# Attention and feed-forward on one core: the second layer's M1 copied to a second bank pair and accumulated on, early value products and the first pair's normalising at other places

## The chip, the cores and the metric

One core of one Trainium2 chip runs the whole kernel. The metric is the device time of one execution in microseconds, as the median of several runs; less is better.

## The reference, cut to what matters

```python
# q, k, v: (batch 8, heads 8, seq 576, head_dim 64)
scores = q @ k.T / 8
# heads 0-3 see 0 <= i-j < 32; heads 4-7 see 0 <= i-j < 128 with (i-j) % 4 == 0
attn = softmax(where(mask, scores, -1e9))
x = (attn @ v).transpose(0, 2, 1, 3).reshape(4608, 512)
h = x @ w_in                            # 512 -> 2048
g = 0.5 * h * (1 + erf(h / sqrt(2)))    # gelu
out = g @ w_out                         # 2048 -> 512
```

## The kernel before, in words

The 4608 tokens are nine chunks of 512. Attention makes the x of a chunk in four pieces (`part` 0 to 3: qk loads, scores, exp, sums, normalising, a transposition `turned` that is partly done by DMA, the value products, and `xout`, which writes x). All matmuls of the feed-forward layers take each operand as a high part rounded to the fp32r format and a low remainder, and issue three terms (high x high, low x high, high x low).

Chunks 0, 1 and 2 go through the two layers directly: `ffn_h_part` (matmul at line 604) for x @ w_in into PSUM bank 4 or 5, `ffn_gelu` (gelu on ACT at L611, a cast of the high part on ACT at L106, a subtraction on DVE for the low part), and `ffn_o` (matmul at L627) into banks 0 to 3. Their order is a string written by hand, `SCHEDULE` (lines 51 to 73): a word such as `h0.2` stands for one step (feature block 0, part 2), `av0.2` for the value products of chunk 0 (`av_wide`, matmul at L500), `scores1.0` for those of L292 and L306, `av1.3` for L518, `o10` for the twelve L627 matmuls of feature block 10, `split2`, `rest2`, `high2` for cutting the weights of block 2 into high and low parts. The word `:a` or `:d` says which engine takes the step.

Chunks 3 to 8 go in three pairs, (3,4), (5,6) and (8,7), by a scheme of seven products in place of eight blocks. Each pair has four units (a quarter of the weights each), and each unit has 28 products: 14 of the first layer (H), then 14 of the second (O), M1 to M7 in two halves each. A product is six matmuls of 128x128 on 128x512 (line 1036, `product`). Weight pieces come through a ring of five tiles filled by DMA (`ring_load`, L991, issued on SP). The first layer's operands B11, B21, B22, T1 to T4 are made by `combine` (casts on ACT at L915, subtractions on DVE at L920). In the second layer, `operands` does the same from the gelu outputs: casts of the high parts on ACT (L1082), low parts on DVE (L1083), and the differences T1 (L1084), T3 (L1085), T2 (L1086) and T4 (L1087) on DVE. `first_layer` makes the gelu inputs (L1065 and L1068 on DVE) and runs the gelu on ACT (L1066, L1067, L1069); line 1061 copies the first layer's M1 to a second bank.

[...] In the second layer the seven products of a unit rotate over three bank pairs, `OBANKS`: M1 in (0,1), M3 in (2,3), M5 in (4,5), M2 in (0,1), M7 in (2,3), M6 in (0,1), M4 in (4,5). Each is drained by `drains` on DVE (L1096 copies for the first unit, L1098 adds to the SBUF totals for the later ones), seven drains per unit, each of 128x1024. After a pair's last unit `final` combines the seven totals by seven additions (L1112; on POOL for the first two pairs, on DVE before the closing unit of the last pair) and sends outT by DMA from SP (L1109). The very last unit, the closing one, has an order and drains of its own (`last_drains`), and already copies and accumulates.

Every step of the paired part is entered by `add(at, rank, step)` at a time in ticks (one tick is one product); `upto` emits them by time, then rank, between the products. An engine runs its instructions in the order in which they are emitted; SP is the queue from which nearly all DMAs are issued, in that order. For the pieces of the next pair's attention, `attend` takes a dict of times, `begin` for the first pair's first piece.

Of the kernel before, what the change touches and what calls it, by code (L numbers as in the profile page):

```python
# [39 lines left out]
BANK0 = (4, 0, 2, 6)  # L40

# [15 lines left out]
turn0.3 half0.2.0:a half0.2.1:a av0.0 half0.3.1:a high0.1:d half0.3.0:a rest1 w2 qk1.0 high1:a rest1 x0.0:a x0.1:a  # L57
x0.0 x0.1 av0.2 x0.2:a h0.0 h0.1 x0.3:a x0.2 qk1.1 h1.0 h1.1 x0.3 h0.2 h0.3 mid3 split2 h0 split2 h1.2 split2 w3
h1.3 rest2 h0:a scores1.0 rest2 high2:a h0 h1 h1:a h2 split3 w4 mid5 low1.0 split3 o0 low1.0:a h2 split3 mid4 h2:a
# [8 lines left out]
rest12 turn1.3:a h10 turn1.2:a high12:d join13.1 rest12 av1.2 h11 split13 mid14 h11:a split13 h12 av1.3   # L68
h11 x1.2:a join15.0 w14 x1.2 split13 o10 x1.3:a h12 x1.3 h12:a keep0 rest13 join15.1 h12 o11 rest13 high13:a
# [17 lines left out]
def attn_ffn(ctx: ExitStack, tc: tile.TileContext, qk, qk_lp, qk_ld, v, v_ld, w, outT):  # L87
    nc = tc.nc
# [402 lines left out]
    def av_wide(s, o):  # L491

        yield "p"
        for a in range(2):
            for r in range(4):
                c0 = (2 * r + a) * 2 * KB
                for y, g, e, cols in sorted([(y, *x) for y in (s, o) for x in parted(y)], key=lambda x: (x[2], x[1])):
                    t = y.t[:, (2 * (g % 2) + a) * 4 + r]
                    bank = BANK0[s.p + e] + 1
# [219 lines left out]
    for token in SCHEDULE.split():  # L719
# [3 lines left out]
        if name == "fill":  # L723
            bank = 7
# [178 lines left out]
    def combine(c, z, at):  # L903
# [34 lines left out]
        B11=(0, -13, -12.4), B21=(0, -11.5, -10.9), T1=(-8.6, -7.8, -7), B22=(0, -2.4, -1.6), T3=(-4.6, -3.8, -3.2), T2=(-5.4, -4.9, -4.2),  # L938
        T4=(-3.5, -3, -2.5)).items()})
# [58 lines left out]
    SLOT = dict(B11=0, T3=0, B22=1, T2=1, T1=2, T4=2, B21=3)  # L998
# [314 lines left out]
```

## Time and profile before

| what | value |
|---|---|
| time of three runs | 855.35, 856.35, 861.83 us; median 856.35 us |
| the profiled execution | 852.99 us, of which the span of instructions is 851.1 us |
| mean granted TensorE clock over the span | 0.992 |
| instructions in the span | 19932 |
| busy share PE, DVE, ACT, POOL | 96%, 72%, 55%, 12% |

PE is the matmul engine (TensorE), PEld its weight loads, DVE the vector engine, ACT the scalar engine, POOL GpSimd, SP the engine that issues DMAs. "idle before" is the time in which an engine had nothing to run ahead of a group of rows, and behind the arrow stands what ended it; "issue" means that no semaphore event of the profile explains the wait. One counting rule matters below: an instruction of the program on plain fp32 operands (lines 306, 500, 518 and 572) runs as two matmuls in the trace, so 64 such instructions of the order are 128 of the trace. Those of lines 292, 604, 627 and 1036 count alike in both. Each matmul of the trace has one weight load beside it.

### The profile page before, as it was taken

How to read it: one execution, taken by the hardware profiler on the slowest of the kernel's cores; microseconds unless marked ns; L12 is line 12 of the kernel's file. 1: busy time of each engine (PE TensorE's matmuls, PEld its weight loads, DVE VectorE, ACT ScalarE, POOL GpSimd, SP SyncE). 2: the span in 40 equal slices, each digit the busy share in tenths (PEclk: the TensorE clock that was granted, in tenths of full speed). 3: DMA queues.
4: the chain of work that ended last, by engine and by line, in shares of the span. 5: the costliest groups of instructions: out<-in, count | busy, mean ns of one | idle time of the engine just before them, and what ended most of it. 6: DMA issues, size and time to landing. Idle time of an engine off the chain costs nothing.

```text
span 851.1 us, 19932 instructions
## 1 busy us (share of the span) xinstructions
PE 817.4 (96%) x8400; PEld 664.3 (78%) x8400; DVE 615.8 (72%) x703; ACT 465.7 (55%) x1089; POOL 103.0 (12%) x94
## 2 busy tenths in 40 slices
PE   6799989999998999899999999999999999999997
PEld 5587868887786888788888877787888777888885
DVE  7597962435765579585959799966767898483977
ACT  7477823454766357473737574646665635244242
POOL 2000002052302630000000018000000064000000
PEclk9999999999999999999999999999999999999999
DMA  9997367984599847967777777876667668566664
GB/s 359 418 418 281 115 199 298 382 302 154 206 332 349 317 160 254 317 223 235 249 225 264 235 273 227 282 261 200 213 204 234 204 206 269 182 195 195 197 197 150
DMA packets 118295, 212.30 MB, mean 249 GB/s; under 512 B 6848, under 2 KB 92864, under 8 KB 110784
## 3 DMA queue, kind: packets, MB, share of 16 engines
q1 hardware_dynamic: 118064, 210.79, 71.7%
q8 instruction: 66, 1.08, 0.5%
q10 hardware_dynamic: 144, 0.26, 0.1%
q14 instruction: 21, 0.17, 0.1%
HBM read 161.21 MB, written 42.99 MB: 240 GB/s over the span
## 4 chain that ended last, share of the span: by engine, by line
PE 73%; DVE 11%; DMA 7%; issue 3%; ACT 3%; SPq 2%; DVEq 0%; ACTq 0%
PE ps L1036 40%; PE ps L604 14%; PE ps L627 12%; DMA turned<-turned 3%; PE ps L306 2%; DVE g L1083 2%; PE ps L572 2%; DMA raw_w<-w 2%; DMA outT<-o_sb 1%; DVE acc L1098 1%; DVE xc L920 1%; DMA v_sb<-v 1%; SPq L382 1%; PE ps L529 1%; DMA ring<-wd 1%
## 5 line engine op out<-in xcount | busy, mean ns | idle before, releaser
L1036 PE MATMUL ps<-xc,ring 128*128 128x512 f32 x1008 | 239.2, 395 | 0.0
L1036 PE MATMUL ps<-g,ring 128*128 128x512 f32 x1008 | 233.3, 391 | 0.8 <-DVE g L1083 0.7
L1036 PEld LDWEIGHTS ps<-xc,ring 128*128 128x128 f32 x1008 | 189.8, 190 | 41.8 <-DVE acc L1098 0.6
L1036 PEld LDWEIGHTS ps<-g,ring 128*128 128x128 f32 x1008 | 188.1, 188 | 43.3 <-DVE g L1083 3.4
L1083 DVE TENSOR_TENSOR g<-g_value,g 128x1024 fp32r<-128x1024 f32 x84 | 106.5, 1277 | 75.9 <-ACT g L1082 75.9
L604 PE MATMUL ps<-x,weight 128*128 128x512 f32 x576 | 138.0, 394 | 2.0 <-issue 2.0
L627 PE MATMUL ps<-g,weight 128*128 128x512 f32 x576 | 137.0, 395 | 1.5 <-issue 1.5
L627 PEld LDWEIGHTS ps<-g,weight 128*128 128x128 f32 x576 | 108.5, 190 | 25.3 <-issue 2.4
L604 PEld LDWEIGHTS ps<-x,weight 128*128 128x128 f32 x576 | 107.2, 188 | 25.6 <-issue 2.9
L1082 ACT CAST g<-g_value 128x1024 fp32r<-128x1024 f32 x84 | 87.1, 1046 | 36.9 <-DVE g_value L1084 20.1
L1112 POOL TENSOR_TENSOR acc<-acc 128x1024 f32<-128x1024 f32 x14 | 44.2, 3169 | 348.2 <-DVE acc L1098 347.7
L616 DVE TENSOR_TENSOR g<-gf,g 128x512 fp32r<-128x512 f32 x48 | 34.3, 715 | 61.2 <-ACT g L106 61.2
L1098 DVE TENSOR_TENSOR acc<-ps,acc 128x1024 f32<-128x1024 f32 x56 | 67.5, 1217 | 13.6 <-PE ps L1036 13.6
L427 ACT ACTIVATE sm<-sm,st 128x64 f32<-128x64 f32 (+1 forms) x224 | 75.4, 338 | 0.2
L611 ACT ACTIVATE gf<-ps 128x512 f32<-128x512 f32 x48 | 28.7, 598 | 81.1 <-PE ps L604 81.0
L783 POOL TENSOR_TENSOR whole<-weight 128x512 f32<-128x512 f32 x32 | 47.2, 1508 | 134.0 <-DMA sd<-sums 54.5
L1061 ACT COPY ps<-ps 128x512 f32<-128x512 f32 x24 | 13.7, 570 | 78.2 <-PE ps L1036 78.2
L1057 ACT COPY u<-ps 128x512 f32<-128x512 f32 x48 | 28.1, 586 | 32.9 <-PE ps L1036 29.3
L427 ACT ACTIVATION_READ_ACCUMULATOR sm<-sm,st 128x1 f32 x224 | 42.1, 188 | 0.0
L920 DVE TENSOR_TENSOR xc<-xn,xc 128x1024 fp32r<-128x1024 f32 x21 | 34.9, 1682 | 8.5 <-ACT xc L915 8.5
L1066 ACT ACTIVATE g_value<-g_value 128x512 f32<-128x512 f32 x24 | 15.1, 632 | 44.6 <-DVE g_value L1065 44.6
L306 PEld LDWEIGHTS ps<-raw_qk 64*32 64x32 f32 x2304 | 26.2, 110 | 12.0 <-issue 4.0
(124 smaller groups left out, 792.6 us busy)
## 6 DMA issues: line engine op xcount, KB each, us to landing
ring<-sd SPq DMA_DIRECT2D x96, 512.0 KB, 4.3
ring<-wd SPq DMA_DIRECT2D x72, 512.0 KB, 4.3
v_sb<-v SPq DMA_DIRECT2D x17, 1024.0 KB, 7.2
raw_qk<-qk SPq DMA_DIRECT2D x32, 512.0 KB, 7.6
wd<-weight SPq DMA_DIRECT2D x16, 1024.0 KB, 10.1
sd<-sums SPq DMA_DIRECT2D x16, 1024.0 KB, 6.0
raw_w<-w SPq DMA_DIRECT2D x15, 1024.0 KB, 17.1
weight<-wd SPq DMA_DIRECT2D x8, 1024.0 KB, 8.6
```

The source lines that it names most:

```text
L306: nc.tensor.matmul(s.sc[32 * r:32 * r + 32, h, c0:c0 + s.nk], x[:, q0:q0 + 32], x[:, k0:k0 + s.nk], start=s.c > 1, stop=s.c > 1 or u == NU ...
L427: nc.scalar.activation(t, s.sc[:, h, at:at + 2 * KB] if s.c < 2 else t, AF.Exp, bias=st[:, 0], scale=SCALE if s.c < 2 else -1.0, accum_out ...
L604: nc.tensor.matmul(bank, weights[f][:, t, cc * P:(cc + 1) * P], x[:, xx], start=n == 1 and i == 0, stop=n == parts and i == 2)
L616: nc.vector.tensor_sub(g[:, 1], gf, g[:, 0])
L627: nc.tensor.matmul(ps[:, d], weights[f][:, t, DM + d * P:DM + (d + 1) * P], gs[f][:, u], start=f == first and n == 0, stop=f == last and n ...
L783: nc.gpsimd.tensor_add(to, x, y)
L920: nc.vector.tensor_sub(combined[k][:, :, 1], part(*VALUE[k]), combined[k][:, :, 0])
L1036: nc.tensor.matmul(ps[:, bank], lhs, rhs, start=start and i == 0, stop=i == 5, skip_group_check=True)
L1082: add(base + t, 4, run("a", lambda k=k, v=v: nc.scalar.copy(operand(k, 0, final), val(v))))
L1083: add(base + t1, 4, run("d", lambda k=k, v=v: sub(operand(k, 1, final), val(v), operand(k, 0, final))))
L1098: plus(total(m), src, total(m))
L1112: add(base + dt * n, 6, run(e[n], lambda g=g, to=to, x=x, y=y: g.tensor_add(total(to), total(x), total(y))))
```

## The change

Four things are done, all on the order of work and the banks; the values computed are the same.

1. In the hand-written `SCHEDULE`, twelve of the first L604 matmuls (h0.0, h0.1, h1.0, h1.1) go ahead of `av0.2`, `scores1.0` goes ahead of the next L604 matmuls, and splits of weight block 2 go ahead of `x0.2`. The bank of chunk 0's wide value products is taken from a table of its own, `XBANK0`.
2. In the same string `av1.3` goes behind `o10`.
3. The normalising of the first pair's first attention piece goes from 0.2 to -2.8 ticks, and three low parts of `combine(3, 4)` go from before tick 0 to ticks 1.6, 3.2 and 5.
4. In the second layer of every unit but the closing one, ACT copies M1 from banks (0,1) to (2,3); M2 is accumulated on that copy and M6 on M1 itself. M1 has no drain of its own any more; six drains stay. The order of the products becomes M1, M3, M2, M5, M6, M7, M4, their operands are made in another order, and `final` has five additions in place of seven; the total of M2 needs none and is sent out by itself, at two ticks before the additions.

```diff
+XBANK0 = (5, 1, 3, 2)
@@ SCHEDULE, around the first L604 matmuls
-turn0.3 half0.2.0:a half0.2.1:a av0.0 half0.3.1:a high0.1:d half0.3.0:a rest1 w2 qk1.0 high1:a rest1 x0.0:a x0.1:a
-x0.0 x0.1 av0.2 x0.2:a h0.0 h0.1 x0.3:a x0.2 qk1.1 h1.0 h1.1 x0.3 h0.2 h0.3 mid3 split2 h0 split2 h1.2 split2 w3
-h1.3 rest2 h0:a scores1.0 rest2 high2:a h0 h1 h1:a h2 split3 w4 mid5 low1.0 split3 o0 low1.0:a h2 split3 mid4 h2:a
+turn0.3 half0.2.0:a half0.2.1:a av0.0 half0.3.1:a high0.1:d half0.3.0:a rest1 w2 qk1.0 qk1.1 high1:a rest1 x0.0:a
+x0.1:a x0.0 x0.1 h0.0 h0.1 h1.0 h1.1 split2 av0.2 x0.2:a split2 x0.3:a split2 scores1.0 x0.2 x0.3 h0.2 h0.3 mid3
+h0 h1.2 w3 h1.3 rest2 h0:a rest2 high2:a h0 h1 h1:a h2 split3 w4 mid5 low1.0 split3 o0 low1.0:a h2 split3 mid4 h2:a
@@ SCHEDULE, the last value products of chunk 1
-rest12 turn1.3:a h10 turn1.2:a high12:d join13.1 rest12 av1.2 h11 split13 mid14 h11:a split13 h12 av1.3 
-h11 x1.2:a join15.0 w14 x1.2 split13 o10 x1.3:a h12 x1.3 h12:a keep0 rest13 join15.1 h12 o11 rest13 high13:a
+rest12 turn1.3:a h10 turn1.2:a high12:d join13.1 rest12 av1.2 h11 split13 mid14 h11:a split13 h12
+h11 join15.0 w14 split13 o10 av1.3 x1.2:a h12 x1.2 x1.3:a h12:a x1.3 keep0 rest13 join15.1 h12 o11 rest13 high13:a
@@ the first pair
-        begin = H01 if j else dict(qk=-17, scores=-10, low=-9.6, exp=(-7.8, -6.2), every=.2, norm=0.2, swap=2.1, v=-3, av=9.2, back=(9.6, 10.4))
+        begin = H01 if j else dict(qk=-17, scores=-10, low=-9.6, exp=(-7.8, -6.2), every=.2, norm=-2.8, swap=2.1, v=-3, av=9.2, back=(9.6, 10.4))
-        B11=(0, -13, -12.4), B21=(0, -11.5, -10.9), T1=(-8.6, -7.8, -7), B22=(0, -2.4, -1.6), T3=(-4.6, -3.8, -3.2), T2=(-5.4, -4.9, -4.2),
-        T4=(-3.5, -3, -2.5)).items()})
+        B11=(0, -13, -12.4), B21=(0, -11.5, -10.9), T1=(-8.6, -7.8, -7), B22=(0, -2.4, 3.2), T3=(-4.6, -3.8, 1.6), T2=(-5.4, -4.9, -4.2),
+        T4=(-3.5, -3, 5)).items()})
@@ the second layer of the pairs
-    OSEQ = tuple((m, e) for m in ("M1", "M3", "M5", "M2", "M7", "M6", "M4") for e in range(2))
+    OSEQ = tuple((m, e) for m in ("M1", "M3", "M2", "M5", "M6", "M7", "M4") for e in range(2))
-    A, B_, C = (4, 5), (0, 1), (2, 3)
-    OBANKS = (B_, C, A, B_, C, B_, A)
+    FIRST, COPY, OTHER = (0, 1), (2, 3), (4, 5)
+    OBANK = dict(M1=FIRST, M3=OTHER, M2=COPY, M5=OTHER, M6=FIRST, M7=COPY, M4=OTHER)
-    SLOT = dict(B11=0, T3=0, B22=1, T2=1, T1=2, T4=2, B21=3)
+    SLOT = dict(B11=0, T2=0, B22=1, T3=1, T1=2, B21=3, T4=3)
@@ operands
-            plan = [("B11", 7.5, 8.5), ("B22", 11.1, 11.9), ("T1", 13.2, 15.2), ("B21", 15.1, 16.4), ("T3", 16.2, 18.4), ("T2", 18.3, 20.3), ("T4", 20.6, 22.4)]
-            at = (12.6, 13.3, 14.9, 18.2)
+            plan = [("B11", 7.5, 8.5), ("B22", 11.1, 11.9), ("B21", 14.9, 15.9), ("T1", 14.2, 17.1), ("T2", 16.4, 18.8), ("T3", 18.2, 20.8), ("T4", 20.2, 22.4)]
+            at = (12.6, 14.4, 14.9, 17.6)
@@ drains
-        for n, b in enumerate(OBANKS):
-            m = OSEQ[2 * n][0]
+        for e in range(2):
+            add(base + 15 + e, 2, run("a", lambda e=e: nc.scalar.copy(ps[:, COPY[e]], ps[:, FIRST[e]])))
+        for n, m in enumerate(("M3", "M2", "M5", "M6", "M7", "M4")):
...
-            add(base + (16, 18, 23, 22, 24, 26, 28)[n], 2, run("d", fn))
+            add(base + 18 + 2 * n, 2, run("d", fn))
-    FINAL = (("M2", "M1", "M2"), ("M6", "M1", "M6"), ("M7", "M6", "M7"), ("M6", "M6", "M5"), ("M5", "M7", "M5"), ("M3", "M6", "M3"), ("M4", "M7", "M4"))
+    FINAL = (("M5", "M5", "M6"), ("M3", "M3", "M5"), ("M6", "M6", "M7"), ("M4", "M4", "M6"), ("M5", "M5", "M7"))
@@ final
+        if pair:
+            add(base - 2, 6, run("q", lambda: out("M2")))
@@ the loop over the products
-            bank, start = OBANKS[(k - QT // 2) // 2][y], True
+            bank, start = OBANK[x][y], x not in ("M2", "M6")
```

On PE, near the start: the value products of chunk 0 (L500 before, L501 in the changed file), the first-layer matmuls (L604, L605), the scores of chunk 1 (L292 and L306, L293 and L307) and the second layer's first matmuls (L627, L628). Before:

```order
L500 MATMUL ps<-zeroed,v_sb 32x64 x128
L604 MATMUL ps<-x,weight 128x512 x24
L292 MATMUL ps<-early 128x256 x2
L306 MATMUL ps<-raw_qk 32x64 x32
L292 MATMUL ps<-early 128x256 x2
L306 MATMUL ps<-raw_qk 32x64 x32
L604 MATMUL ps<-x,weight 128x512 x12
L627 MATMUL ps<-g,weight 128x512 x24
```

and with the change:

```order
L501 MATMUL ps<-zeroed,v_sb 32x64 x64
L605 MATMUL ps<-x,weight 128x512 x12
L501 MATMUL ps<-zeroed,v_sb 32x64 x64
L293 MATMUL ps<-early 128x256 x2
L307 MATMUL ps<-raw_qk 32x64 x32
L293 MATMUL ps<-early 128x256 x2
L307 MATMUL ps<-raw_qk 32x64 x32
L605 MATMUL ps<-x,weight 128x512 x24
L628 MATMUL ps<-g,weight 128x512 x24
```

Half of the value products now stand behind twelve first-layer matmuls, and the scores stand ahead of the other 24 instead of between 24 and 12.

On SP, at the start of the first pair: outT stores of chunk 2, the DMA swaps that finish the transposition (`turned`, L382 before, L383 in the changed file) and loads of the weight ring (L991). Before:

```order
L641 DMA outT<-o_sb 128x512 x3
L382 DMA turned<-turned 32x512 x2
L991 DMA ring<-sd_139 128x4x256
L382 DMA turned<-turned 32x512 x4
L991 DMA ring<-wd_1_134 128x4x256
L382 DMA turned<-turned 32x512 x2
L991 DMA ring<-wd_0_133 128x4x256
```

and with the change:

```order
L642 DMA outT<-o_sb 128x512 x2
L383 DMA turned<-turned 32x512 x2
L642 DMA outT<-o_sb 128x512
L383 DMA turned<-turned 32x512 x6
L991 DMA ring<-sd_139 128x4x256
L991 DMA ring<-wd_1_134 128x4x256
L991 DMA ring<-wd_0_133 128x4x256
```

The eight swaps, which were spread over two ring loads, stand ahead of both.

On DVE, in the second half of a unit of the third pair, which has no attention beside it: T1 (L1084), the gelu inputs (L1068), T3 (L1085), T2 (L1086), T4 (L1087), the low parts (L1083) and the drains (L1098 before, L1100 in the changed file). Before:

```order
L1084 TENSOR_TENSOR g_value<-g_value 128x1024
L1068 TENSOR_TENSOR g_value<-ps,u 128x512
L1085 TENSOR_TENSOR g_value<-g_value 128x1024
L1068 TENSOR_TENSOR g_value<-ps,u 128x512
L1086 TENSOR_TENSOR g_value<-g_value 128x1024
L1083 TENSOR_TENSOR g<-g_value,g 128x2x512
L1098 TENSOR_TENSOR acc<-ps,acc 128x1024
L1083 TENSOR_TENSOR g<-g_value,g 128x2x512
L1098 TENSOR_TENSOR acc<-ps,acc 128x1024
L1087 TENSOR_TENSOR g_value<-g_value 128x1024
L1083 TENSOR_TENSOR g<-g_value,g 128x2x512 x2
```

and with the change:

```order
L1084 TENSOR_TENSOR g_value<-g_value 128x1024
L1068 TENSOR_TENSOR g_value<-ps,u 128x512 x2
L1085 TENSOR_TENSOR g_value<-g_value 128x1024
L1086 TENSOR_TENSOR g_value<-g_value 128x1024
L1083 TENSOR_TENSOR g<-g_value,g 128x2x512 x2
L1087 TENSOR_TENSOR g_value<-g_value 128x1024
L1100 TENSOR_TENSOR acc<-ps,acc 128x1024
L1083 TENSOR_TENSOR g<-g_value,g 128x2x512
L1100 TENSOR_TENSOR acc<-ps,acc 128x1024
L1083 TENSOR_TENSOR g<-g_value,g 128x2x512
```

The drain of M1, the first L1098 before, is gone; the first drain is now that of M3, behind eight other instructions counted from T1.

## Rows read from the trace of the kernel before

**Rows 1.** The profile page: busy time of PE (share of the span, instructions), and the DMA queue of kind "instruction" (packets, MB, share of 16 engines).
```profile
PE 817.4 (96%) x8400; PEld 664.3 (78%) x8400; DVE 615.8 (72%) x703; ACT 465.7 (55%) x1089; POOL 103.0 (12%) x94
...
q8 instruction: 66, 1.08, 0.5%
```

**Rows 2.** The waits of PE over the whole span: the line that waited, what ended the wait, us in total, times, longest us.
```profile
PE ps L572 <- DMA turned<-turned: 5.0, 6, 1.8
PE ps L518 <- issue: 4.2, 2, 3.8
PE ps L500 <- issue: 3.8, 1, 3.8
...
PE ps L306 <- DVE xn L585: 1.5, 2, 0.9
...
PE ps L1036 <- DVE g L1083: 0.7, 1, 0.7
```

**Rows 3.** The timeline of PE from 22 to 46 us: start, us, engine, line, operation, tiles, shape, count, and the idle time before it.
```profile
28.09 2.73 PE L500 MATMUL ps<-zeroed,v_sb 128*32 128x64 f32 x125 [3.76 <-issue]
...
34.38 5.06 PE L604 MATMUL ps<-x,weight 128*128 128x512 f32 x21 [1.98 <-issue]
39.28 0.40 PE L292 MATMUL ps<-early 128*128 128x256 f32 x2
...
41.61 3.01 PE L604 MATMUL ps<-x,weight 128*128 128x512 f32 x12
44.46 1.75 PE L627 MATMUL ps<-g,weight 128*128 128x512 f32 x7
```

**Rows 4.** The DMA view of three stretches, 34.4 to 37.9, 37.9 to 39.0 and 111.4 to 112.4 us: queue and kind, packets, MB, share of 16 engines. In the first stretch q1 is the only queue.
```profile
q1 hardware_dynamic: 202, 1.48, 101.7%
...
q8 instruction: 1, 0.02, 6.1%
...
q8 instruction: 1, 0.02, 5.5%
```

**Rows 5.** Windows of the trace: stretch, its length, busy time and count of PE, PEld, DVE, ACT, POOL, then the granted TensorE clock (1.00 is full), the DMA share and GB/s.
```profile
29.40:32.70 3.30, 3.00 (x58) 2.02 (x46) 1.44 (x3) 2.04 (x3) 0.00 (x0) 0.50 1.02 419
...
114.80:118.10 3.30, 3.30 (x9) 2.61 (x8) 2.97 (x5) 3.27 (x6) 0.00 (x0) 0.50 0.03 5
360.50:363.80 3.30, 3.30 (x30) 2.55 (x12) 0.78 (x2) 0.00 (x0) 0.00 (x0) 0.50 0.23 79
538.00:541.30 3.30, 3.30 (x10) 2.53 (x9) 3.23 (x4) 1.37 (x3) 0.00 (x0) 0.50 1.05 383
```

**Rows 6.** The timeline of ACT from 38 us on: the gelu of feature block 0, its cast, and the cast of weight block 2.
```profile
38.12 0.60 ACT L611 ACTIVATE gf<-ps 128x512 f32<-128x512 f32 x1 [5.10 <-PE ps L604]
38.75 0.62 ACT L106 CAST g<-gf 128x512 fp32r<-128x512 f32 x1
39.27 1.17 ACT L106 CAST weight<-raw_w 128x1024 fp32r<-128x1024 f32 x1
```

**Rows 7.** The timeline of PE from 104.7 to 122 us: the value products av1.2 and av1.3 (L518) with first- and second-layer matmuls.
```profile
104.75 1.40 PE L518 MATMUL ps<-turned,v_sb 64*32 64x32 f32 x128
106.08 3.01 PE L604 MATMUL ps<-x,weight 128*128 128x512 f32 x12
...
113.87 0.61 PE L518 MATMUL ps<-turned,v_sb 64*32 64x32 f32 x43 [3.85 <-issue]
114.40 7.33 PE L627 MATMUL ps<-g,weight 128*128 128x512 f32 x24
```

**Rows 8.** The timeline of PE at the first pair's first value products (L572).
```profile
356.49 0.32 PE L572 MATMUL ps<-v_sb,turned 64*32 64x64 f32 x8
357.22 0.44 PE L572 MATMUL ps<-v_sb,turned 64*32 64x64 f32 x16 [0.41 <-DMA turned<-turned]
359.48 1.37 PE L572 MATMUL ps<-v_sb,turned 64*32 64x64 f32 x104 [1.82 <-DMA turned<-turned]
```

**Rows 9.** The timeline of DVE ahead of it: low parts of `combine`, and the transposition that the swaps wait for.
```profile
340.74 3.49 DVE L920 TENSOR_TENSOR xc<-xn,xc 128x1024 fp32r<-128x1024 f32 x3
...
345.90 1.25 DVE L374 STREAM_TRANSPOSE turned<-sm 128x1024 f32<-128x1024 f32 x1
```

**Rows 10.** The timeline of SP's DMA issues in the same stretch: start, us that the issuing took.
```profile
349.61 4.12 SPq L382 DMA_DIRECT2D turned<-turned  x4
...
354.54 1.26 SPq L382 DMA_DIRECT2D turned<-turned  x2
```

**Rows 11.** The timeline of DVE in the second layer of a unit of the third pair.
```profile
749.39 1.22 DVE L1084 TENSOR_TENSOR g_value<-g_value 128x1024 f32<-128x1024 f32 x1
750.53 0.68 DVE L1068 TENSOR_TENSOR g_value<-ps,u 128x512 f32<-128x512 f32 x1
751.13 1.21 DVE L1085 TENSOR_TENSOR g_value<-g_value 128x1024 f32<-128x1024 f32 x1
```

**Rows 12.** The timeline of ACT in the same unit: the copies that follow its first two products, and two casts of operands.
```profile
733.08 0.57 ACT L1061 COPY ps<-ps 128x512 f32<-128x512 f32 x1 [9.54 <-PE ps L1036]
734.44 0.57 ACT L1061 COPY ps<-ps 128x512 f32<-128x512 f32 x1 [0.79 <-PE ps L1036]
...
753.64 2.00 ACT L1082 CAST g<-g_value 128x1024 fp32r<-128x1024 f32 x2
```

**Rows 13.** Timelines of POOL and DVE: six of the POOL additions after the first pair, one DVE instruction beside them, and the same DVE instruction at a time without POOL work.
```profile
513.91 19.06 POOL L1112 TENSOR_TENSOR acc<-acc 128x1024 f32<-128x1024 f32 x6 [2.40 <-DVE acc L1098]
...
517.51 3.21 DVE L367 TENSOR_TENSOR sm<-sm,st 128x1024 f32<-128x1024 f32 x1
...
652.27 1.23 DVE L367 TENSOR_TENSOR sm<-sm,st 128x1024 f32<-128x1024 f32 x1
```

More of the change, by code (lines that the diff above doesn't have):

```diff
@@ L498, in av_wide @@
                     t = y.t[:, (2 * (g % 2) + a) * 4 + r]
-                    bank = BANK0[s.p + e] + 1
+                    bank = XBANK0[s.p + e]
                     nc.tensor.matmul(ps[32 * g:32 * g + 32, bank, c0:c0 + 2 * KB], y.v[:, a, r, cols],
@@ L535, in xout @@
         if s.c < 2:
-            px = ps[:, s.bank + 1] if s.wide_v else ps[:, s.bank:s.bank + 2, s.p % 2 * 256:s.p % 2 * 256 + 256]
+            px = ps[:, XBANK0[s.p]] if s.wide_v else ps[:, s.bank:s.bank + 2, s.p % 2 * 256:s.p % 2 * 256 + 256]
             to = [s.x[:, t] if s.wide_v else s.x[:, t].rearrange("p (k n) -> p k n", k=2) for t in range(2)]
@@ L958, in attn_ffn @@
             (0, "M3"), (1, "M3"), (0, "M4"), (1, "M4"))
-    OSEQ = tuple((m, e) for m in ("M1", "M3", "M5", "M2", "M7", "M6", "M4") for e in range(2))
+    OSEQ = tuple((m, e) for m in ("M1", "M3", "M2", "M5", "M6", "M7", "M4") for e in range(2))
     LSEQ = tuple((m, e) for m in ("M1", "M3", "M2", "M6", "M5", "M7", "M4") for e in range(2))
-    A, B_, C = (4, 5), (0, 1), (2, 3)
-    OBANKS = (B_, C, A, B_, C, B_, A)
-    LBANKS = (B_, C, B_, C, B_, C, A)
+    FIRST, COPY, OTHER = (0, 1), (2, 3), (4, 5)
+    OBANK = dict(M1=FIRST, M3=OTHER, M2=COPY, M5=OTHER, M6=FIRST, M7=COPY, M4=OTHER)
     X_OF = dict(M1="B11", M2="B21", M3="B22", M4="T4", M5="T1", M6="T2", M7="T3")
@@ L1089, in drains, with fn @@
     def drains(base, q):
-        for n, b in enumerate(OBANKS):
-            m = OSEQ[2 * n][0]
-            def fn(b=b, m=m):
-                src = ps[:, b[0]:b[0] + 2]
+        for e in range(2):
+            add(base + 15 + e, 2, run("a", lambda e=e: nc.scalar.copy(ps[:, COPY[e]], ps[:, FIRST[e]])))
+        for n, m in enumerate(("M3", "M2", "M5", "M6", "M7", "M4")):
+            def fn(m=m):
+                b = OBANK[m][0]
+                src = ps[:, b:b + 2]
                 if q == 0:
@@ L1112, in final @@
             add(base + dt * n, 6, run(e[n], lambda g=g, to=to, x=x, y=y: g.tensor_add(total(to), total(x), total(y))))
-            if pair and to in PLACE:
+            if pair and n in (1, 3, 4):
                 add(base + dt * n + .1, 6, run("q", lambda to=to: out(to)))
@@ L1155, in attn_ffn @@
             if closing(j, q):
-                final(base + .3, 1, None, "ddddddd")
+                final(base + 1.3, 1.2, None, "ddddd")
                 last_drains(base, PAIRS[j])
@@ L1160, in attn_ffn @@
         if j < NPP - 1:
-            final(base + QT + 1, 2, PAIRS[j], "ggggggg")
+            final(base + QT + 1, 2, PAIRS[j], "ggggg")
     steps.sort(key=lambda t: t[:3])
```

## The prediction

> **What bounds the kernel now.** I began with the page: PE is busy for 817.4 of 851.1 us [rows 1]. A change of order can win only from PE's idle time and from stretches in which PE runs at half clock; what delays PE costs in full. The changed kernel issues as many matmuls as before, so the whole forecast is a count of PE's stalls. Then I read PE's waits: the largest causes are swaps of `turned` (5.0 us in 6), two "issue" waits of 3.8 us and, smaller, DVE results late for L306 and L1036 [rows 2]. Third, the timeline around each of those that the change touches [rows 3, 7, 8]. [...]
>
> The "issue" waits need a cause. Queue q8, of kind instruction, brought 66 packets of 1.08 MB together [rows 1]: 16.4 KB each, and 16,800 matmuls and loads of PE over 66 is 255 instructions for a packet, some 127 matmuls. The stalls at 28.09 and 34.38 are 125 + 3 = 128 matmuls apart (three of the 24 of L604 ran before the second) [rows 3]. In 37.9 to 39.0 and in 111.4 to 112.4 one such packet came in, and PE resumed 1.5 us after the latter, at 113.87 [rows 4, 7]; in 34.4 to 37.9 other DMAs filled the engines (101.7%) and none came [rows 4]. So I take it that one block of 128 matmuls is fetched ahead, that the fetch is asked for when the block before it is entered, and that it comes late when DMA is full. A block of L604 or L627 matmuls takes 128 x 0.24 = 31 us (0.24 is 2.85 us from 41.61 to 44.46 over 12 [rows 3]) and hides that; a block of short attention matmuls takes 2 to 3 us and does not.
>
> [...]
>
> **A. Early value products and scores: +3.5 us.** Up to 34.38 both orders use up the same two blocks, so the stalls of 3.76 and 1.98 stay. Before, the third block then held 21 long matmuls, which hid its successor's fetch. Now it holds 9 matmuls of L501 and 119 of the scores: 0.2 + 119/132 of 2.33 us (39.28 to 41.61 [rows 3]) = 2.3 us. PE stands at the block's end at 36.7, and the next block can be used at 39.0 + 1.5 = 40.5 [rows 4]: a new stall of 3.8 us. A stall of 3.76 was followed by half clock after 1.3 us [rows 3, 5], so I charge that too. After 40.5 come 13 scores (0.2) and 24 L605 (24 x 0.24 = 5.7), then 1.65 for the clock: 48.0, where PE stood at 44.46 before. The last 12 of the 24 wait for feature block 0's gelu, its cast and the weight cast, 2.32 us on ACT [rows 6] that the scores used to cover, against six matmuls now; at half clock these take 2.9 us and cover it, so it costs nothing beside the slow stretch. Bounds: no stall and full clock, but that ACT wait exposed (2.32 + 0.3 - 1.4 = 1.2), gives 34.38 + 0.2 + 2.33 + 5.7 + 1.2 = 43.8, -0.6; both losses and a fetch 1.5 us later give +6.2.
>
> **B. `av1.3` behind `o10`: -4.3 us.** Before, PE reached a block's end at 110.02, stood for 3.85 us, and ran at half clock from 114.8 [rows 5, 7]. Now 12 L628 matmuls (12 x 0.24 = 2.8 us) stand ahead of av1.3. They need only the gelu of block 10, which stands ahead of h11 in the schedule. The fetch is asked for at the same instruction, so PE arrives at 110.02 + 2.8 less the 12 value matmuls that fall behind the edge (0.15) = 112.7 and waits 1.2. That saves 2.65, and, as the stall is short, the 1.65 of half clock. Bounds: all of it gone, -5.5; the slow stretch stays and the fetch comes 1.6 us later, -1.0. The DMAs that `join15` and `w14` issue do not move past a swap.
>
> **C. First pair's normalising: -3.9 us.** PE waits 0.41 + 1.82 for swaps and then has half clock [rows 5, 8]: 3.88 us. The transposition at 345.90 stood behind three low parts (3.49 us at 340.74) [rows 9]; these now come later, and it ends near 343.7. On SP, the last swaps were issued by 355.8 behind two ring loads [rows 10]. Now the eight stand together: those at 349.61 took 1.03 each, so all are out by 343.7 + 8.2 = 351.9, and with the 3.7 us that the last took before (355.8 to 359.48) they land by 355.6, ahead of PE at 356.49. The ring load that they pass goes out 0.6 us later; no wait of PE on the ring stands in rows 2. The three low parts at 1.6 to 5 ticks serve products M3 and M4 of the unit, ticks 10 to 13. Bounds: -3.9 and 0.
>
> **D. M5 behind M3's drain: +6.8 us.** This is the new wait. M5 uses the banks of M3, two products later, and its first matmul (tick 20) waits for M3's drain; behind it stand all products, and PE has nothing else. DVE takes 1.14 us for a 128x1024 instruction (749.39 to 750.53) and 0.60 for a 128x512 one [rows 11]. From T1 at 749.39: two gelu inputs to 751.73, T3 to 752.86, T2 to 754.0. B21's low part waits for its cast on ACT (after the second gelu, some 754.5; the cast pair of before ran 753.64 to 755.64 [rows 12]). Then B21 low, T1 low and T4 end at 757.9, and the drain ends at 757.92 + 1.21 = 759.1. PE, at 1.36 us a product (733.08 to 734.44 [rows 12]), reaches tick 20 at 758.7. So 0.45 us a unit. Eleven units have this; seven plain ones 3.2 us, the other four, where DVE also runs attention and low parts of the next pair, some 0.7 to 1.0 each: 3.6. Bounds: nothing, if the queue runs 0.5 earlier, and one whole drain per unit, 11 x 1.21 = 13.3.
> The drain that goes (M1's) saves PE nothing, since DVE wasn't waited for there. The two new copies, 0.57 each [rows 12], stand behind B21's cast and end at 755.6, before M2 wants the bank at 756.2: nothing, by 0.6 us of cover.
>
> [...]
>
> **E. Fewer additions on POOL: -3.0 us.** While POOL adds (19.06 us for six [rows 13]), a DVE multiplication takes 3.21 us in place of 1.23 [rows 13]. That made L306 wait 1.5 us for DVE and was followed by half clock at 538 [rows 2, 5]: 3.2 us. Five additions that start one drain later, in place of seven, cover less of it. The 0.7 of L1036 on DVE [rows 2], beside the second pair's additions, goes too. Against that, `turned` swaps after the first pair now stand behind M2's and M3's stores on SP: 0.9 us. Bounds: -3.9, and +1.5 where the slow instructions only move.
>
> **Sum.** 3.5 - 4.3 - 3.9 + 6.8 - 3.0 = -0.9 on the profiled 852.99, so 852.1. The median of the runs before, 856.35, is 3.36 above that execution; hence 855.5. About 1% (8.5 us) is what a measurement of this kernel tells from no change.
>
> **Rivals.**
> 1. The early stalls are no fetches but belong to the instructions that stand there. For: the profile names no cause. Against: the spacing of 128 and the packets. Then A gives back 3.76 + 1.98 + 1.65 less 1.2 = -6.2, and B its 5.5 in full: 855.5 - 9.7 - 1.2 = 844.6. Chance 0.13.
> 2. M3's drain is in time, D near +1: T1 or the cast comes 0.5 us earlier. For: the miss is 0.45 in a queue of eight. Against: the queue is tied to product 13 through L1068. 849.7. Chance 0.20.
> 3. C fails: the swaps go out early and still land late, as in the other five waits on them [rows 2]. 859.4. Chance 0.09.
> 4. The slower side: DVE's queue ahead of M3's drain is one instruction longer in each unit. ACT's chain before B21's low part (two gelus, T1's cast, B21's cast) has no slack, and each 1.14 us it slips goes through T1 low, T4 and the drain to PE: 11 x 1.14 = 12.5, 868.0. It decides from 0.8 us a unit on (9.5 us over eleven). Against: ACT idles between these casts. Chance 0.12.
>
> The forecast has 0.46; its own range is 850 to 861. Faster by over 1% (below 847.8): rival 1 and 0.02 of rival 2, 0.15. Slower (above 864.9): rival 4 and 0.01 of rival 3, 0.13. Within 1%: 0.72. A range of 844.5 to 863 holds rivals 1 to 3 and the forecast, and leaves rival 4 out.
>
> **What would show it.** A: a PE wait on "issue" near 37 to 40 in the scores. B: an issue wait of about 1.2 in L519 near 113, without half clock behind. C: no wait for `turned` near 357. D: waits of L1036 on the drain (acc, DVE) of 0.3 to 1 in nearly every unit, some 6.8 together; if they are under 2, rival 2 is right, if above 15, rival 4. E: no half clock near 538. I am wrong in the cause of the early stalls if in the changed kernel they don't stand 128 matmuls apart.

## The result, and the profile after

The changed kernel is slower: 863.96 us median (861.72 to 868.18, 11 runs), against 859.21 us for the kernel before on the same chips (853.5 to 861.91, 11 runs). The ratio is 1.0069, 95% interval 1.0042 to 1.0097, some 6 us. Forecast were 855.5 us and a range of 844.5 to 863: no change that can be told, and the range missed by 1 us. Its profiled execution took 862.84 us with a span of 861.0, near its median. That of before (852.99) turned out to lie low: in later sets of 20 to 35 runs its kernel had medians of 856.5 to 861.0. The ratios here and below leave out as slow what lies over 1.5% above the fastest run of the same kernel: among the changed kernels that is one of e13's nine runs and four of e6's 12, and over all 12 e6's median is 861.40 us, against 861.02 for all runs of before beside it.

The page after: PE is busy for 5.5 us more and idle for 4.4 us more than before [rows 1].

```profile
PE 822.9 (96%) x8400; PEld 664.6 (77%) x8400; DVE 599.9 (70%) x690; ACT 475.0 (55%) x1111; POOL 91.2 (11%) x90
```

The waits of PE after, to be laid beside [rows 2]:

```profile
PE ps L573 <- issue: 5.9, 3, 3.7
...
PE ps L307 <- issue: 3.1, 1, 3.1
...
PE ps L605 <- ACT weight L107: 1.9, 2, 1.6
PE ps L1036 <- DVE acc L1100: 1.8, 4, 0.8
...
PE ps L519 <- issue: 1.4, 1, 1.4
PE ps L1036 <- ACT ps L1091: 1.4, 2, 0.7
```

Three kinds of wait are new: for a weight cast on ACT, for drains (`acc`) and for the copies of M1 (L1091). The stall of av1.3 fell from 3.85 to 1.4 us, that of L307 on DVE (`xn`, 1.5) is gone, and the value products of the pairs (L573) have issue stalls of 5.9 us, 3.7 of them in one place.

**The early part.** The timeline of PE, beside [rows 3]:

```profile
36.85 0.74 PE L307 MATMUL ps<-raw_qk 64*32 64x64 f32 x51
40.65 0.34 PE L307 MATMUL ps<-raw_qk 64*32 64x64 f32 x13 [3.06 <-issue]
40.91 4.62 PE L605 MATMUL ps<-x,weight 128*128 128x512 f32 x12
45.83 3.02 PE L605 MATMUL ps<-x,weight 128*128 128x512 f32 x12 [0.29 <-ACT weight L107]
48.68 1.52 PE L628 MATMUL ps<-g,weight 128*128 128x512 f32 x6
```

The scores run dry with 13 matmuls left, as counted from the blocks. The second layer starts at 48.68 instead of 44.46: +4.2. The stalls before it did not stay, as step A has them, at 3.76 and 1.98: the change has one of 1.46 us at 28.43 and none at the next block's edge, and runs at half clock in between (below). The stalls at 28.43 and 40.65 stand 255 matmuls apart, two blocks, so step A's sign of a wrong cause did not come.

**av1.3.** PE, beside [rows 7], and ACT in the same stretch:

```profile
115.45 0.88 PE L519 MATMUL ps<-turned,v_sb 64*32 64x32 f32 x73
117.78 0.74 PE L519 MATMUL ps<-turned,v_sb 64*32 64x32 f32 x55 [1.44 <-issue]
118.44 3.02 PE L628 MATMUL ps<-g,weight 128*128 128x512 f32 x12
123.02 3.37 PE L605 MATMUL ps<-x,weight 128*128 128x512 f32 x12 [1.56 <-ACT weight L107]
```

```profile
118.55 0.59 ACT L107 CAST x<-ps 128x512 fp32r<-128x512 f32 x1 [7.78 <-PE ps L519]
...
121.84 1.12 ACT L107 CAST weight<-raw_w 128x1024 fp32r<-128x1024 f32 x1
```

ACT stands idle for 7.78 us in front of the cast of x, which waits for av1.3, and the weight cast is queued behind it. av1.3 now ends 4 us later, so the cast does, and PE waits for it.

**The first pair's value products**, beside [rows 8], run without a wait:

```profile
360.01 1.51 PE L573 MATMUL ps<-v_sb,turned 64*32 64x64 f32 x128
```

**The second layer.** Units are counted from 0 to 11 over the three pairs. The unit of [rows 11] is unit 9. PE ran through its second layer without a gap before:

```profile
750.56 19.20 PE L1036 MATMUL ps<-g,ring 128*128 128x512 f32 x84
```

DVE and PE in that unit after:

```profile
765.60 1.22 DVE L1087 TENSOR_TENSOR g_value<-g_value 128x1024 f32<-128x1024 f32 x1
766.74 1.22 DVE L1100 TENSOR_TENSOR acc<-ps,acc 128x1024 f32<-128x1024 f32 x1
```

```profile
765.76 1.98 PE L1036 MATMUL ps<-g,ring 128*128 128x512 f32 x8
768.01 3.25 PE L1036 MATMUL ps<-g,ring 128*128 128x512 f32 x13 [0.27 <-DVE acc L1100]
```

M3's drain ends at 767.96 and M5 starts at 768.01. The unit's products 14 to 20, with this wait of 0.27 among them, take 0.43 us longer than before, and to 24 another 0.13. In units 0 to 6, where attention runs beside it, the second copy of M1 stands behind other work on ACT; this is unit 5:

```profile
594.14 0.57 ACT L1091 COPY ps<-ps 128x512 f32<-128x512 f32 x1
594.72 1.28 ACT L428 ACT_TABLE_LOAD   x1
596.02 0.35 ACT L428 ACTIVATE sm<-sm,st 128x64 f32<-128x64 f32 x1
...
596.70 0.57 ACT L1091 COPY ps<-ps 128x512 f32<-128x512 f32 x1
```

Between the two copies lies an activation table load of 1.28 us and part of a softmax, and the second half of M2 waits 0.71 for its bank. In unit 4 that wait is 0.64. In unit 0 the second copy starts at 374.73, behind a table load too, and ends at 375.31; M2's second half starts at 375.35, 0.17 us late, and M2 takes some 0.3 us more in all.

**A stall that nobody forecast**, at the value products of the second pair's third attention piece, first before, then after:

```profile
622.81 1.73 PE L572 MATMUL ps<-v_sb,turned 64*32 64x64 f32 x128
```

```profile
625.42 1.46 PE L573 MATMUL ps<-v_sb,turned 64*32 64x64 f32 x124
630.61 0.30 PE L573 MATMUL ps<-v_sb,turned 64*32 64x64 f32 x4 [3.73 <-issue]
```

The DMA view of the changed kernel in 621.0 to 628.1 and in 628.1 to 629.4 us (queue, packets, MB, share):

```profile
q1 hardware_dynamic: 1742, 1.79, 80.2%
...
q8 instruction: 1, 0.02, 5.2%
```

The first stretch holds no instruction packet. It came only when most of the other traffic was over (q1 at 5.7% of the second stretch), at 628.1 or later; PE went on at 630.61. In the kernel before, a packet came in 618.3 to 619.9, ahead of the same value products. The granted clock after:

```profile
27.80:34.50 6.70, 6.07 (x98) 4.84 (x102) 2.43 (x3) 0.00 (x0) 0.00 (x0) 0.50 1.02 419
41.50:44.70 3.20, 3.20 (x9) 2.47 (x8) 0.00 (x0) 1.17 (x3) 0.00 (x0) 0.50 1.02 420
115.00:118.40 3.40, 1.96 (x131) 1.49 (x129) 0.00 (x0) 0.00 (x0) 0.00 (x0) 1.00 0.35 142
...
632.00:635.20 3.20, 3.20 (x9) 2.50 (x8) 1.38 (x3) 0.63 (x1) 0.00 (x0) 0.50 0.27 74
```

```profile
533.00:536.30 3.30, 3.30 (x74) 2.65 (x67) 0.78 (x2) 0.00 (x0) 0.00 (x0) 0.50 0.99 313
```

Beside [rows 5]: no half clock behind av1.3 any more, but one at 533 behind a swap wait of 1.6 us in place of the one at 538, a new one at 632 behind the new stall, and 6.7 us of it in the early part in place of 3.3.

### The profile page after: what moved, and what is told of

Read it like the earlier page. It is cut to its first block, busy times and chain, and to the rows that moved or that the text cites. A ratio compares the mean times of both kernels' runs of the same rounds, so it can differ in the third digit from the quotient of the medians.

```text
span 861.0 us, 19923 instructions
## 1 busy us (share of the span) xinstructions
PE 822.9 (96%) x8400; PEld 664.6 (77%) x8400; DVE 599.9 (70%) x690; ACT 475.0 (55%) x1111; POOL 91.2 (11%) x90
## 4 chain that ended last, share of the span: by engine, by line
PE 70%; DVE 13%; ACT 7%; DMA 4%; issue 3%; SPq 1%; DVEq 0%; ACTq 0%
PE ps L1036 38%; PE ps L605 14%; PE ps L628 12%; PE ps L307 3%; DVE g L1083 2%; DMA turned<-turned 2%; PE ps L573 2%; ACT g L1082 1%; ACT sm L428 1%; DMA raw_qk<-qk 1%; DVE acc L1100 1%; DMA v_sb<-v 1%; SPq L383 1%; DVE g_value L1084 1%; DVE g_value L1087 1%
## 5 line engine op out<-in xcount | busy, mean ns | idle before, releaser
L1036 PE MATMUL ps<-g,ring 128*128 128x512 f32 x1008 | 237.4, 392 | 4.3 <-DVE acc L1100 1.8
L1083 DVE TENSOR_TENSOR g<-g_value,g 128x1024 fp32r<-128x1024 f32 x84 | 102.6, 1232 | 79.3 <-ACT g L1082 79.3
L605 PE MATMUL ps<-x,weight 128*128 128x512 f32 x576 | 141.6, 400 | 4.4 <-ACT weight L107 1.9
L628 PE MATMUL ps<-g,weight 128*128 128x512 f32 x576 | 135.4, 391 | 1.8 <-issue 1.8
L605 PEld LDWEIGHTS ps<-x,weight 128*128 128x128 f32 x576 | 108.8, 192 | 29.9 <-ACT weight L107 2.7
L628 PEld LDWEIGHTS ps<-g,weight 128*128 128x128 f32 x576 | 107.5, 188 | 24.8 <-issue 2.2
L1100 DVE TENSOR_TENSOR acc<-ps,acc 128x1024 f32<-128x1024 f32 x48 | 58.6, 1220 | 21.5 <-PE ps L1036 21.5
L1116 POOL TENSOR_TENSOR acc<-acc 128x1024 f32<-128x1024 f32 x10 | 32.1, 3222 | 359.8 <-DVE acc L1100 359.5
L921 DVE TENSOR_TENSOR xc<-xn,xc 128x1024 fp32r<-128x1024 f32 x21 | 32.8, 1578 | 8.5 <-ACT xc L916 8.4
L307 PEld LDWEIGHTS ps<-raw_qk 64*32 64x32 f32 x2304 | 26.2, 110 | 13.5 <-issue 7.9
```

Source lines behind the costliest of these rows:

```text
L307: nc.tensor.matmul(s.sc[32 * r:32 * r + 32, h, c0:c0 + s.nk], x[:, q0:q0 + 32], x[:, k0:k0 + s.nk], start=s.c > 1, stop=s.c > 1 or u == NU ...
L605: nc.tensor.matmul(bank, weights[f][:, t, cc * P:(cc + 1) * P], x[:, xx], start=n == 1 and i == 0, stop=n == parts and i == 2)
L628: nc.tensor.matmul(ps[:, d], weights[f][:, t, DM + d * P:DM + (d + 1) * P], gs[f][:, u], start=f == first and n == 0, stop=f == last and n ...
L921: nc.vector.tensor_sub(combined[k][:, :, 1], part(*VALUE[k]), combined[k][:, :, 0])
L1036: nc.tensor.matmul(ps[:, bank], lhs, rhs, start=start and i == 0, stop=i == 5, skip_group_check=True)
L1083: add(base + t1, 4, run("d", lambda k=k, v=v: sub(operand(k, 1, final), val(v), operand(k, 0, final))))
```

## The experiments

Ratios are to the kernel before, with 95% intervals; a thousandth is 0.86 us.

| run | what | ratio | interval |
|---|---|---|---|
| the change | all of it | 1.0069 | 1.0042 to 1.0097 |
| e1 | early order alone | 1.0037 | 1.0012 to 1.0062 |
| e2 | av1.3 alone | 0.9983 | 0.9964 to 1.0003 |
| e3 | normalising alone | 0.9961 | 0.9934 to 0.9987 |
| e4 | second layer alone | 1.0113 | 1.0088 to 1.0139 |
| e5 | change, third piece normalised earlier | 1.0068 | 1.0031 to 1.0105 |
| e6 | change, drain ahead of T4 | 0.9983 | 0.9946 to 1.0020 |
| e7 | change, weight 13 cut earlier | 1.0025 | 0.9992 to 1.0058 |
| e8 | av1.3 with weight 13, normalising | 0.9939 | 0.9905 to 0.9972 |
| e11 | before, five POOL additions | 0.9959 | 0.9929 to 0.9989 |
| e12 | change without early order, with both mends | 0.9985 | 0.9956 to 1.0015 |
| e13 | second layer alone, drain ahead of T4 | 1.0069 | 1.0036 to 1.0103 |
| e14 | change, value products three products later | 1.0027 | 0.9999 to 1.0054 |
| e15 | e8 with these value products later | 0.9900 | 0.9863 to 0.9937 |

**e1 to e4: each part alone**, by its hunks of the diff.

> Only the early value products and scores are moved (and the bank table that goes with them); av1.3, the normalising and the second layer stay as before. Theory (instruction fetch, one block of 128 matmuls ahead): the scores again run dry after 119 of their 132 matmuls, PE waits some 3 us on issue near 40 us, half clock follows, and L628's first matmul comes 4.2 us later than before; the time is some 4 us above the kernel before (ratio about 1.005). Rival (the early stalls belong to the instructions that stand there): no new stall, and 6 us less.

Measured +3.2 us (1.0037). Its trace has the stall in the same place, 2.7 us with 13 scores left, and L628's first matmul 4.6 us later than before. The fetch theory holds, the rival falls.

> Only av1.3 goes behind o10. By the prediction -4.3 us. By the trace of the changed kernel the fetch stall falls to 1.4 us and the half clock goes, but the cast of the next weights stands on ACT behind the cast of x1.2, which waits for av1.3, and PE waits 1.6 us for it: -1.8 us. If that wait comes only together with the early move, nothing of it is seen here and -4.3 us is right.

Measured -1.5 us, with an interval that still holds no change, and PE's wait of 1.6 us for the weight cast is there without the early order. In its own trace the fetch stall of av1.3 is gone altogether, and past the wait for the weight cast PE is 3.2 us ahead of the kernel before.

> Only the first pair's normalising and the low parts of combine move. Prediction: no wait for turned near 357, no half clock behind it, -3.9 us (the changed kernel showed -4.3). Rival: the swaps still land late, 0.

Measured -3.3 us; the gain of the trace (-4.3 up to the end of that layer) was kept in this part.

> Only the second layer: M1 copied, M2 and M6 accumulated, M1's drain gone, five final additions. Prediction: L1036 waits for M3's drain 0.4 to 0.5 us in each plain unit and about 1 in units with attention, 6.8 us together; fewer POOL additions give back some of it (-3.0 predicted, -1.4 in the changed kernel): +4 to +5.5 us. Rival (the accumulation costs nothing and the slowdown of the changed kernel is a fetch stall of 3.7 us at the third pair's value products that comes in some executions only): 0 to -2 us.

Measured +9.7 us, nearly twice the higher expectation. So most of the loss of the whole change lies here. Its trace has D's waits, the copies' waits of 1.4 us, and the issue stall at the third piece's value products (3.2 us).

**e5: is that stall a matter of the swaps?**

```diff
-        attend(z, 0, base, later(H01, 2 * QT))
+        attend(z, 0, base, later(dict(H01, norm=-1.8) if j == 1 else H01, 2 * QT))
```

> The changed kernel, with the normalising of the second pair's third attention piece 2 ticks earlier, so that its swaps are not issued next to three ring loads just before the value products at 630 us. Theory (the new 3.7 us issue stall of L573 there is an instruction fetch that comes behind a DMA burst, which the second layer's other timing brings about): stall and half clock behind it go, 5 us less than the changed kernel, some 858 to 859 us. Rival (the stall belongs to the second layer in another way, or to chance): it stays in the trace, and the time is that of the changed kernel, 864.

1.0068, and a stall of 4.0 us in the trace: issuing the swaps earlier does not help. That the swaps' place makes the fetch late is refuted.

**e6: the drain ahead of T4**

```diff
-            at = (12.6, 14.4, 14.9, 17.6)
+            at = (12.6, 14.4, 14.9, 18.1)
```

> The changed kernel, with the difference T4 put behind M3's drain on DVE, so that the drain ends 1.14 us earlier and M5's first matmul finds its bank free. Prediction's step D: the waits of L1036 on acc (0.43 a plain unit, about 1 in units 3, 4 and 7) go in the plain units and shrink by 1.1 at most elsewhere, 5 to 6.5 us less than the changed kernel, 858 us. Rival: the cost per unit is that of the accumulation itself or of the ACT copies, and moving the drain changes less than 2 us.

0.9983, 7.4 us under the change by the two ratios. In its trace DVE and PE of the unit shown above read

```profile
759.38 1.22 DVE L1100 TENSOR_TENSOR acc<-ps,acc 128x1024 f32<-128x1024 f32 x1
760.52 1.22 DVE L1087 TENSOR_TENSOR g_value<-g_value 128x1024 f32<-128x1024 f32 x1
```

```profile
754.79 9.46 PE L1036 MATMUL ps<-g,ring 128*128 128x512 f32 x41
```

The drain is done 1.14 us earlier, and 41 matmuls run through without a gap; no wait on `acc` is left among the larger ones of this trace. That PE waited for this drain is shown. How much it cost the runs tell only roughly: in the traces the products 14 to 24 of the eleven units take 4.7 us less than in the change. Part of the 7.4 is not D: this profiled execution has only 0.2 us of the stall at the third piece.

**e7: weight block 13 cut earlier**

```diff
-... split13 o10 av1.3 x1.2:a h12 x1.2 x1.3:a h12:a x1.3 keep0 rest13 join15.1 h12 o11 rest13 high13:a
+... split13 o10 rest13 rest13 high13:a av1.3 x1.2:a h12 x1.2 x1.3:a h12:a x1.3 keep0 join15.1 h12 o11
```

> The changed kernel, with the cutting of weight block 13 into high and low parts (two rest steps and the high cast on ACT) ahead of av1.3 instead of behind the casts of x1.2 and x1.3, which wait for av1.3. Theory: PE's wait of 1.56 us on the weight cast at 123 us goes, 1.6 us less than the changed kernel. Rival: another operand is late next (gelu or its cast for block 12), and nothing is won.

1.0025. The wait on the cast is gone in the trace, but the next weights' low part on DVE is late one block further on (0.94 us), so that some 1.3 us of the 1.6 stay won there. The ratio says 3.8 us less than the change, within the two intervals of either.

**e8: the two parts that gain, with that mend**

> The kernel before with the two parts that gained alone: av1.3 behind o10 (with weight block 13 cut ahead of it) and the first pair's normalising earlier; the early order and the second layer stay as before. Sum of the single parts: -1.5 - 1.6 - 3.3 = -6.4 us against the kernel before, ratio 0.9925. Rival: the gains overlap or are given back at the next fetch, -2 to -3 us.

0.9939, -5.2 us (-8.2 to -2.4). That is about the sum of e2 and e3, -4.8; a further gain by weight block 13 can't be told from none.

**e9: the kernel before once more**, one execution.

> The kernel before, unchanged, once more with a profile. Theory: the profiled execution of before (852.99) was one in which two fetches came in time that come late in others: at the 45th block, near 490 us, and at the 57th, at the value products near 624 us. A second profile then shows one or both as issue waits of 1 to 4 us, with a span 3 to 8 us longer, though nothing was changed. Rival: the span is again near 851 and both are absent, and the late fetches of the other kernels are owed to their edits.

857.32 us, span 855.4, 4.4 us above the first profile of the same kernel. Of the two fetches one was late (0.8 us), the other not; 2.6 us had come up by the second layer's first matmul, with an early stall of 3.3 us where [rows 3] has 1.98.

```profile
PE ps L519 <- issue: 4.8, 2, 4.1
...
PE ps L605 <- issue: 3.3, 1, 3.3
...
PE ps L1037 <- issue: 0.8, 1, 0.8
```

So one profile is worth no more than some 4 us, but this run does not settle how often the 57th block's fetch is late in the kernel before.

**e10: 43 more warm-up matmuls**, one execution: `BURN = 97` for 54.

> The kernel before with 97 in place of 54 warm-up matmuls at its start, so that all later matmuls stand 43 places further back in the instruction stream. Theory (blocks of 256 instructions are fetched): the issue stall of av1.3 comes after 42 of its 128 matmuls, where it came after 85, and that of the first value products after 89 of 256, where it came after 131. Rival (the stall belongs to what the instruction works on): 85 and 131 stay.

PE at the first value products and at av1.3:

```profile
23.13 1.47 PE L500 MATMUL ps<-zeroed,v_sb 128*32 128x64 f32 x89
28.39 2.56 PE L500 MATMUL ps<-zeroed,v_sb 128*32 128x64 f32 x127 [3.79 <-issue]
34.96 1.30 PE L500 MATMUL ps<-zeroed,v_sb 128*32 128x64 f32 x40 [4.02 <-issue]
```

```profile
112.76 0.60 PE L518 MATMUL ps<-turned,v_sb 64*32 64x32 f32 x42
117.02 1.03 PE L518 MATMUL ps<-turned,v_sb 64*32 64x32 f32 x86 [3.66 <-issue]
```

89 and 42, to the matmul. The stalls belong to the place in the instruction stream, which settles the first rival. And the run took 876.04 us: with the edges 43 matmuls earlier in the kernel's work, new stalls of 2 to 5.6 us stand in five other places (three of them at L572, 11.2 us), some 20 us in all, by one execution, for a kernel that does the same.

**e11: two POOL additions left out of before**

```diff
+            if pair and n in (2, 3):
+                continue
```

> The kernel before, with two of the seven POOL additions after the first and the second pair left out (those into M7 and the second into M6; this part of the sums is missing from the output), all else as before. Prediction's step E: -3.2 to -3.9 us. Rival: the stalls of L306 on DVE stay or cost nothing, since the half clock near 538 comes and goes without them: 0, within 1.5 us.

-3.5 us. POOL then runs

```profile
519.52 12.31 POOL L1114 TENSOR_TENSOR acc<-acc 128x1024 f32<-128x1024 f32 x4 [2.42 <-DVE acc L1098]
```

in place of 19.06 us [rows 13], and the waits of L306 on DVE (1.5 us) are gone. Step E's size is right where nothing else moves; its trace had the stall at the third piece all the same.

**e12: the change without the early order, both mends in**

> The changed kernel without the early order, with weight block 13 cut ahead of av1.3 and T4 behind M3's drain. From the ratios so far: 0.9939 for the two moves, 1.0113 for the second layer, and 0.9914 for the drain (0.9983 over 1.0069): 0.9965, some 3 us below the kernel before and 2 us above the version with the two moves alone. Rival: without the drain's wait the second layer gains by its shorter DVE queue and POOL work, ratio under 0.9939.

0.9985, 4 us above e8, though the two intervals overlap: no sign that the second layer gains, even with its drain in time. The expectation (0.9965) lies inside the interval.

**e13 to e15: where the rest of the second layer goes.** e13 is e4 with e6's line. e14 and e15 move the value products at 625 us three products later:

```diff
-        attend(z, 0, base, later(H01, 2 * QT))
+        attend(z, 0, base, later(dict(H01, av=12.2, back=(12.6, 13.4)) if j == 1 else H01, 2 * QT))
```

> Only the second layer of the change, with T4 behind M3's drain. The second layer alone was at 1.0113, of which the prediction's D is 6 to 7 us (0.75%). Theory (D is the drain; the rest is ACT's copies in two units, 1.4 us, and a late fetch at the 57th block that comes more often): 1.0035 to 1.005, about 3 to 4 us above the kernel before. Rival (the drain was all of it, and fewer POOL additions pay the predicted 3 us): 0.997 or less.

1.0069, above what was expected (1.0035 to 1.005), though its interval holds nearly all of that: the drain takes 3.8 us off e4 by the ratios, and 5.2 by the two traces, from product 14 to 24 of each unit. The stall at the third piece is in its trace (3.2 us).

> The changed kernel, with the value products of the second pair's third attention piece three products later, so that 20 long and 105 short matmuls stand between the edges of blocks 56 and 57 in place of 2 and 124; the edges themselves stay. Theory (fetch): that block lasts 6 us in place of 2, the stall of 3 to 4 us there and the half clock behind it go, and the time falls by up to 5 us from the changed kernel's ratio of 1.0069 to about 1.002. Rival: the fetch is late whenever these value products run, and the stall moves with them: 1.007.

1.0027, as expected. PE:

```profile
616.27 13.90 PE L1036 MATMUL ps<-xc,ring 128*128 128x512 f32 x60
630.10 1.52 PE L573 MATMUL ps<-v_sb,turned 64*32 64x64 f32 x128
```

By the count the block edge now stands after 105 of the 128, and there is no stall. But this trace does not show that the longer block hid a late fetch, for its fetch was not late. The DMA view of e14 in 621.4 to 623.6 us, as PE entered the block:

```profile
q8 instruction: 1, 0.02, 3.9%
```

In e15's trace too the packet came as PE entered the block (615.8 to 617.5). So the 3.6 us rest on the two ratios, whose intervals overlap a little, and how they were won stays argued. That long matmuls ahead of an edge cover a late packet is shown elsewhere: with 21 of L604 ahead of the edge near 41 us a packet at 37.9 or later cost nothing [rows 3, 4], and with scores in their place PE stood for 3.06 us.

> The version with av1.3 and the normalising moved (0.9939), with the same value products three products later. Its trace had the stall of 3.2 us and half clock at that edge: up to 5 us less, ratio 0.989 to 0.991, if the stall comes in most of its executions; 0.993 if it comes in few.

0.9900 (848.69 us median, 5 runs): the fastest version, better than both kernels. Against e8 it is 3.4 us less, within the two intervals. Three edits of order make it: av1.3 behind o10 with weight 13 cut ahead, the earlier normalising, and these later value products.

## Why the prediction was wrong

The second layer was forecast at +3.8 us (D and E) and measured +9.7 (e4). The step that failed most is one that the sum put at nothing: it counted stalls only where the change moves work, and took the fetches at all other block edges to stay as in one profile. At the edge of block 57 PE then stood for 3 to 4 us in most traces with the new second layer, 3.6 us by e14; that the change makes it more frequent was not shown to be more than chance. M1's copies, put at nothing as well, cost some 2 us. Outside the second layer step B failed: it gave -4.3 us and brought -1.5, for a weight cast behind a cast that waits for av1.3 made PE wait 1.56 us.

- **What bounds it, and the fetch.** Right: e10, with stalls after 89 and 42 matmuls, ties the early ones to the place in the stream, and the packets [rows 4] tie them to the fetch. That each block is asked for as the one before it is entered was the author's reading, and the traces fit it: in the kernel before, the packet for the edge at 624.2 us came at 618.4, about one block ahead, and those of the stalls came later still.
- **A**, forecast +3.5: 1.0037 alone, +3.2 (+4.2 in the trace of the change). Right in place, count and size of the new stall, but not in the two stalls before it, which were to stay: PE passed the second of these edges some 0.6 us later than before, without a stall, after a stretch at half clock.
- **B**, forecast -4.3: -1.5 alone. Step B failed in one sentence, "They need only the gelu of block 10". It looked at what av1.3 is moved past on PE, and not at what stands behind av1.3's reader on ACT: the cast of x1.2 holds up the weight cast for block 13. The fetch stall (1.4 for 1.2) and the clock came as forecast. Over all traces that stall is 3.0 to 4.6 us in the eight with av1.3 in its old place and 0 to 1.7 in the nine with it behind o10.
- **C**, forecast -3.9: -3.3 alone. Right.
- **D**, forecast +6.8: the waits are there, 0.43 + 0.13 us in units 9 and 10, which have no attention beside them (0.45 forecast), and about 1 in units 3 and 7; summed over the eleven units, from product 14 to 24 of each, the two traces differ by 6.9. That this meets the forecast is luck, for it holds the copies too: moving the drain takes 4.7 (e6) and 5.2 us (e13) off that sum. Right in mechanism, with 6.8 forecast for about 5.
- **The copies of M1**, forecast at nothing by 0.6 us of cover: right in units 7 to 10, where they run back to back, wrong in most of units 0 to 6, where attention's table load stands between them on ACT: 1.4 us of waits in units 4 and 5, and some 0.3 in each of units 0, 1, 2 and 6, which e6 leaves there (M2 takes 3.03 us there in unit 0 and 2.72 in the kernel before).
- **E**, forecast -3.0: -3.5 alone (e11). In the change only -1.4 showed up in that stretch, since half clock came a little earlier instead (533 for 538); in the other seven traces with the second layer it is -1.1 to -3.0.
- **What no step had:** the fetch at the edge of block 57, 3 to 4 us and half clock. PE stood there in six of the seven traces with the second layer and these value products in place, and in two of seven without the second layer. e14 and e15 price it at 3.6 and 3.4 us by the ratios. D with the copies (6.9), this fetch (3.6) and E (-1.4) make 9.1, where e4 measured 9.7 (7.5 to 11.9): the second layer's loss, forecast at +3.8, is accounted for.
- **Half clock**, 1.65 us a stretch in the sum: an estimate, half of the 3.3 us at 0.50 [rows 5]. In the kernel before the 24 L627 matmuls behind av1.3 took 7.33 us with such a stretch in them [rows 7], and 24 from 95.61 us on, at a clock of 1.00, took 5.61: 1.72 less.
- **The base.** The sum was made against one profiled execution and lifted by the median of three runs, 856.35. The same kernel's median in the comparison was 859.21. That is 2.9 of the 8.5 us between forecast and measurement; the rest, 5.6, is the change of order itself, -0.9 forecast and +4.75 measured by the medians (5.9 by the ratio).

Open: why the 57th block's fetch is late more often with the second layer. e5 rules out the swaps' place; that six of seven against two of seven is more than chance was not shown. In the 16 traces other than e10's the ring loads and swaps come in much the same burst. The packet came either within 0.6 us after PE had reached the 7171st matmul, some 15 ahead of the block (seven traces, e14's and e15's among them), or 6.5 to 7.8 us after it, as the burst ended (eight); in e6's it was 3.35 us. What tips it was not found. Nor do the single parts add up exactly: +8.1 us against 5.9, within their intervals.

None of the four rivals describes what happened. The fourth had the right sign but another mechanism: DVE's queue was no longer than counted.

## What to carry to other kernels

Where a PE-bound program issues many short matmuls, look in its trace for stalls a fixed count of instructions apart (256 here, 128 matmuls and their loads), and see what stands between two edges: a block of short matmuls alone ran dry here, for 3.06 us, and the one with 21 long ones in it did not. Here ACT stood idle for 7.78 us ahead of the cast of x, which waited for av1.3, the weight cast was queued behind it, and PE waited 1.56 us for that one: follow the readers of a moved step, not only its neighbours. And take two or three profiles of a kernel before a sum of a few microseconds is made against one of them.

## What was not expected of the hardware

- 43 more warm-up matmuls at the start, work that hides under the first loads, cost some 20 us (876.04 in one execution against a median of 856.5), by the place of the block edges.
- Two POOL additions fewer after each of the first two pairs gave 3.5 us (0.9 to 6.1), though POOL is busy for 12% of the span and no wait of PE on POOL stands in the trace.
- The granted clock of the changed kernel stayed at 0.50 for 6.7 us in one piece, from 27.8 to 34.5 us, with waits of 0.85, 0.98 and 1.46 us between 21.1 and 28.4. In the kernel before it stood at 0.50 for 3.3 us there, behind a wait of 3.76.
